# An attention and mixture-of-experts kernel: one small sum on another engine, three blocks in another buffer, and steps of the hand-written order moved

## The chip, the core and the metric

The kernel runs on one core of one Trainium2 chip. The metric is the device time of one execution in microseconds (us), the median of several runs. PE is the matmul engine (TensorE), DVE VectorE, ACT ScalarE, POOL GpSimd; SP only issues transfers. Each engine takes its instructions in the order in which the program lists them and stands at one whose inputs aren't ready.

## What is computed

The reference is multi-head attention with a learned bias from relative positions, followed by a mixture of experts in which each token goes to one expert (cut to what matters):

```python
scores = scale * q @ k.T + bias                      # 4 batches, 8 heads, 576 tokens, head size 64
attn = exp(scores - max(scores)); attn = attn / (sum(attn) + 1e-09)
x = (attn @ v) as [2304 tokens, 512]
logits = x @ w_gate                                  # 8 experts
e = argmax(logits); g = softmax(logits)[e]; o = sigmoid(x @ w_output_gate)[e]
out[token] = g * o * (maximum(x[token] @ w1[e], 0) @ w2[e])
```

## The kernel before

The program has three stages. The first computes the bias and is not touched. The second is attention: 4 batches of 4 pairs of heads, each pair one pass of the loop on line 997. The third is the experts' stage: slots of 288 tokens that share an expert, 8 of them always (`SURE`), more behind conditions.

**Attention.** What the loop issues, and in which order, stands in strings: `FIRST` for the first pass, `ORDER` for the middle ones, `LAST` for the last, `END` for what is left after it. An entry is a letter with a number: `s` makes the scores of one block of 128 rows for one head (matmuls on line 849, then `softmax_rows`: DVE adds the bias and finds the row's maximum on line 829, ACT takes the exponential on line 834 and writes the row sums to `sums`); `t` transposes weights in pieces of 128x128 on PE (lines 886, 898) and copies them from PSUM to `et` (lines 890, 901) on ACT or DVE, by the letter at its end; `a` multiplies them with `v` (line 918, twenty matmuls) and copies the result to `xt` (line 919). A minus sign means the pair before, a plus sign the pair after. All transposes and small products draw their PSUM tile from `psum_t()`, three buffers in rotation; the scores have two buffers of their own (`ps_s`).

**The queue of small work.** `w` and `u` in the strings, and the entries of `SLOT_WORK` in the experts' stage, each call `do_work`, which takes one step of the first generator in `rows`, or else in `work`. A step is the code up to the next `yield`. Behind the last pair of a batch three kinds of generator are queued: `emit_logits` (three per batch; the first of them, `qq == 0`, also makes the reciprocals of the softmax sums, lines 593 and 594; its copy `ls` on line 609 is ACT's), `emit_route` (gate and expert of each token; at its end it queues `emit_x`), and `route_group`, which turns the experts' numbers into lists of row indices for gathering and scattering. It runs once for batches 0 to 2 (part 0) and once for batch 3 (part 1). Its index matmuls are on line 413; their factors are `a2`, made on POOL for part 0 (lines 399 to 404), and `bl`, made on DVE (line 407).

**The x blocks.** `emit_x` transposes a batch's result into five blocks of rows (four of 128, one of 64), multiplies each on DVE by its gate (line 660) and stores it to DRAM from ACT's queue; a block's store is issued in the step of the next block (line 662), the last one's in a step of its own (line 666). In the last batch all five blocks come from the pool `x_p`, tag `x`, two buffers. Slot answers draw from the same two buffers (`new_y`: answers 0 and 1 of a slot; answer 2 has `y2`).

**Into the experts' stage.** `X` in `LAST` issues three gathers of slot 0's rows on POOL (line 497). The eight `y` entries split slot 0's first weights: ACT makes the high half (line 539), POOL subtracts for the low half (line 540, 128x512, SBUF to SBUF). `x` entries are `transpose_x(0, c)`: three transposes of a chunk of slot 0's rows (line 515), a copy on ACT (516), a subtraction on DVE (517).

**A slot** (`body`) has eight groups f0 to f7 of twelve matmuls (line 1110, three PSUM buffers); behind each ACT makes `hh` (1112) and DVE `hl` (1113), and behind every even group `split` makes two halves of a piece of the second weights (ACT line 486, DVE line 487). Then come four output groups d0 to d3 of 24 matmuls (line 1133), each with an ACT copy into `yts[s % 2]` (line 1139). At the end twelve transposes (1152) and three copies (line 1155: DVE, ACT, DVE) give the slot's three answers, which POOL scatters to the output (line 1076). `yts` are two tiles of 128x4x288, in the places (`qt1`, `qs1`) of attention's keys and queries.

Of the kernel before, what the change touches and what calls it, by code (L numbers as in the profile page):

```python
# [9 lines left out]
F32 = mybir.dt.float32  # L10
# [4 lines left out]
ACTF = mybir.ActivationFunctionType  # L15
ALU = mybir.AluOpType
# [4 lines left out]
B, H, S, D = 4, 8, 576, 64  # L21
HID = 32
NPAIR = H // 2
DM, DFF, NE = 512, 1024, 8
# [3 lines left out]
CH = 288  # L28
# [30 lines left out]
)  # L59

END = (
    "t10a- t11d- a1d- x x w a2d- x w x "
)


# [5 lines left out]
ON_ACT = "210210000111121212102110310010201111"  # L71

SLOT_WORK = (
# [61 lines left out]
def attention_moe_kernel(  # L135
# [15 lines left out]
    nc = tc.nc  # L151
    V = nc.vector
# [5 lines left out]
    qx = ctx.enter_context(tc.tile_pool(name="qx", bufs=1))  # L158
    nat = ctx.enter_context(tc.tile_pool(name="nat", bufs=1))
    spl = ctx.enter_context(tc.tile_pool(name="spl", bufs=1))  # L160
    vp = ctx.enter_context(tc.tile_pool(name="vp", bufs=2))
    xt_p = ctx.enter_context(tc.tile_pool(name="xt", bufs=3))
    x_p = ctx.enter_context(tc.tile_pool(name="x", bufs=2))
# [21 lines left out]
    def psum_t():  # L185
        return ps_t.tile([128, 512], F32, name="pt", tag="t")
# [7 lines left out]
    def route_batch(b):  # L194
# [31 lines left out]
        for t in range(t0, t0 + 5):  # L226
# [2 lines left out]
                out=pm[:, t + 1, :], in0=oh[:, t, :], in1=pm[:, 0 if first else t, :], op=ALU.add  # L229
            )  # L230

    gidx = [const.tile([G, n], U32, name=f"gidx{i}") for i, n in enumerate((NGA, NG + 1))]
    sidx = [const.tile([G, n], U32, name=f"sidx{i}") for i, n in enumerate((NGA, NG + 1))]
    ids_a = const.tile([G, NGA], F32, name="ids_a")
# [20 lines left out]
    def route_group(part):  # L255

        if part == 0:
            yield
        P = V if part else nc.gpsimd
        t0, nt = ((0, NTA), (NTA, NT - NTA))[part]  # L260
# [17 lines left out]
            out=cmp, in0=each(rk[:, nt, :], [128, 8, 16]), in1=over(cn("thr"), [128, 8, 16]), op=ALU.is_gt  # L278
# [7 lines left out]
        for i in range(2):  # L286
            cmp = rt.tile([128, 8, 8], F32, name="cmp8", tag="bl")
            V.tensor_tensor(
                out=cmp, in0=cn("inc").rearrange("p (e f) -> p e f", e=8), in1=over(nch[:, i, :], [128, 8, 8]),
# [5 lines left out]
        if part:  # L295
            V.tensor_scalar(
                out=nb, in0=cn("slot")[:, 0:MORE + 1], scalar1=cinc[:, 7:8], scalar2=float(MORE),
                op0=ALU.add, op1=ALU.is_equal,
# [8 lines left out]
        for i in range(2):  # L307
            sl = rt.tile([1, ns, 8], F32, name="sl", tag="a2")
            V.tensor_tensor(
                out=sl, in0=each(cn("slot")[0:1], [1, ns, 8]),  # L310
# [5 lines left out]
        if part:  # L316
# [11 lines left out]
                out=late, in0=ea, scalar=16.0, in1=ea, op0=ALU.is_lt, op1=ALU.mult  # L328
# [55 lines left out]
        for u in range(nt // 5):  # L384
            us = slice(u * 5, u * 5 + 5)
            ge = rt.tile([128, 5, NG + 1], BF16, name="ge", tag="ge")[:, :, 0:ng + 1]
            V.tensor_tensor(
                out=ge, in0=each(pos[:, us], [128, 5, ng + 1]), in1=over(cn("gthr")[:, 0:ng + 1], [128, 5, ng + 1]),
                op=ALU.is_ge,
            )  # L390
            yield
            lo = rt.tile([128, 5], F32, name="lo", tag="lo")
            V.tensor_reduce(out=lo, in_=ge, op=ALU.add, axis=AX.X)
            V.tensor_scalar(out=lo, in0=lo, scalar1=-1.0, scalar2=-float(G), op0=ALU.add, op1=ALU.mult)
            V.tensor_tensor(out=lo, in0=lo, in1=pos[:, us], op=ALU.add)
            if part:
                yield
            a2 = rt.tile([128, 5, 2, NG], BF16, name="a2", tag="a2")[:, :, :, 0:ng]
            P.tensor_tensor(out=ge[:, :, 0:ng], in0=ge[:, :, 0:ng], in1=ge[:, :, 1:ng + 1], op=ALU.subtract)
            for i, nm in enumerate(("tokhi", "toklo")):  # L400
                P.tensor_tensor(
                    out=a2[:, :, i, :], in0=ge[:, :, 0:ng],
                    in1=each(cn(nm)[:, t0 + u * 5:t0 + u * 5 + 5], [128, 5, ng]), op=ALU.mult,
                )
            yield
            bl = rt.tile([128, 5, G], BF16, name="bl", tag="bl")
            V.tensor_tensor(out=bl, in0=each(lo, [128, 5, G]), in1=over(cn("j96"), [128, 5, G]), op=ALU.is_equal)
            yield
            yield
            pi = psum_t()  # L410
            for i in range(2):
                for t in range(5):
                    nc.tensor.matmul(
                        pi[0:G, i * 128:i * 128 + ng], lhsT=bl[:, t, :], rhs=a2[:, t, i, :],
                        start=t == 0, stop=t == 4,
                    )
            V.scalar_tensor_tensor(
                out=ids[:, 0:ng], in0=pi[0:G, 0:ng], scalar=64.0, in1=ids[:, 0:ng], op0=ALU.mult, op1=ALU.add
            )
            V.tensor_tensor(out=ids[:, 0:ng], in0=ids[:, 0:ng], in1=pi[0:G, 128:128 + ng], op=ALU.add)  # L420
            if u < nt // 5 - 1:
                yield
        if part:
            yield
            g, n = 3 * SURE_A, NG - 3 * SURE_A
# [155 lines left out]
    def emit_logits(b, qq):  # L581

        n = 256 if qq < 2 else 64
        pl = psum_t()
        for pr in range(NPAIR):
            nc.tensor.matmul(
                pl[32 * pr:32 * pr + 32, 0:n], lhsT=wgb[:, pr, :], rhs=xt_t[b, qq][:, pr, :],
                start=True, stop=True,
            )
        if qq == 0:  # L590
            rec_t[b] = st_p.tile([128, 5, H], F32, name="rec", tag="rec", bufs=2)
            rec = rec_t[b][:, 0:4, :]
            V.tensor_scalar(out=rec, in0=sums_t[b], scalar1=1e-9, scalar2=None, op0=ALU.add)  # L593
            V.reciprocal(out=rec, in_=rec)
        if qq == 2:

            for hl in range(2):
                nc.tensor.matmul(
                    pl[0:64, 256 + 4 * hl:260 + 4 * hl], lhsT=ident[:, hl * 64:hl * 64 + 64], rhs=sums4_t[b],
                    start=True, stop=True,  # L600
                )
            rec = rec_t[b][0:64, 4, :]
            V.tensor_scalar(
                out=rec.rearrange("p (a t) -> p t a", t=2), in0=pl[0:64, 256:264].rearrange("p (t a) -> p t a", t=2),
                scalar1=1e-9, scalar2=None, op0=ALU.add,
            )
            V.reciprocal(out=rec, in_=rec)
        ls = st_p.tile([128, 256], F32, name="ls", tag="ls", bufs=1)
        nc.scalar.copy(out=ls[:, 0:n], in_=pl[:, 0:n])
        yield  # L610
        if b == B - 2:
            yield
        pt = psum_t()
        if qq < 2:
            for i in range(2):
                nc.tensor.transpose(pt[:, i * 128:i * 128 + 128], ls[:, i * 128:i * 128 + 128], ident)
            lt = st_p.tile([128, 2 * H, 16], F32, name="lt", tag="ls", bufs=1)
            rb = rec_t[b][:, 2 * qq:2 * qq + 2, :].rearrange("p t h -> p (t h)")
            V.tensor_tensor(
                out=lt, in0=pt[:, 0:256].rearrange("p (h e) -> p h e", e=16), in1=each(rb, [128, 2 * H, 16]),  # L620
                op=ALU.mult,
            )
            t = b * 5 + 2 * qq
            V.tensor_reduce(
                out=logits[:, t:t + 2, :], in_=lt.rearrange("p (t h) e -> p t e h", t=2), op=ALU.add, axis=AX.X
            )
        else:
            nc.tensor.transpose(pt[0:64, 0:128], ls[:, 0:64], ident)
            lt = st_p.tile([128, 2 * H, 16], F32, name="lt", tag="ls", bufs=1)[0:64, 0:H, :]
            V.tensor_tensor(  # L630
                out=lt, in0=pt[0:64, 0:128].rearrange("p (h e) -> p h e", e=16),
                in1=each(rec_t[b][0:64, 4, :], [64, H, 16]), op=ALU.mult,
            )
            V.tensor_reduce(
                out=logits[0:64, b * 5 + 4, :], in_=lt.rearrange("p h e -> p e h"), op=ALU.add, axis=AX.X
            )
# [9 lines left out]
    def emit_x(b):  # L646

        stored = None
        for qb in range(5):
            n = 128 if qb < 4 else 64  # L650
            xt = xt_t[b, qb // 2]
            c0 = (qb % 2) * 128 if qb < 4 else 0
            pt = psum_t()
            for pr in range(NPAIR):
                nc.tensor.transpose(pt[0:n, pr * 128:pr * 128 + 128], xt[:, pr, c0:c0 + n], ident)  # L655

            p, tag = (spl, "hl"[qb // 2]) if qb % 2 and b < B - 1 else (x_p, "x")
            x = p.tile([128, H, D], F32, name="x", tag=tag)
            p3 = pt[0:n].rearrange("p (h d) -> p h d", h=H)
            V.tensor_tensor(out=x[0:n], in0=p3, in1=each(rec_t[b][0:n, qb, :], [n, H, D]), op=ALU.mult)  # L660
            if stored:
                nc.scalar.dma_start(**stored)
            r0 = b * S + qb * 128
            stored = dict(out=x_dram[r0:r0 + n, :], in_=x[0:n].rearrange("p h d -> p (h d)"))
            yield
        nc.scalar.dma_start(**stored)
# [392 lines left out]
    with ExitStack() as ctx:  # L1059
# [6 lines left out]
        w2l = [wr.tile([128, 2, DM], F32R, name=f"w2l{i}") for i in range(4)]  # L1066
        hh_all, hl_all = (hp.tile([128, 8, CH], F32R, name=t) for t in ("hh", "hl"))
        hh, hl = ([t[:, i, :] for i in range(8)] for t in (hh_all, hl_all))
        yts = [qx.tile([128, 4, CH], F32, name=f"yt{t}", tag=t) for t in ("qt1", "qs1")]

        few.append(xt_p.tile([128, 4, FEW], F32, name="few", tag="xt1", bufs=2))
        puts = []
# [183 lines left out]
```

## Time and profile before

| | us |
|---|---|
| median of three runs | 630.18 (629.33 to 630.48) |
| profiled execution, its own time | 629.59 |
| its span, first to last instruction | 627.7 |
| PE busy | 580.1 (92%) |
| DVE busy | 420.2 (67%) |
| ACT busy | 374.7 (60%) |
| POOL busy | 95.3 (15%) |

All times in the rows are from the start of the span. Attention ends and slot 0 begins at about 380 us; slot 1 begins at about 413, and each later slot takes 28 us. A busy PE is not a PE at its best: a matmul at half the granted clock counts as busy too.

### The profile page before, as it was taken

What the parts mean: (1) busy time and instruction counts of PE and PEld (TensorE: products, weight loads), DVE (VectorE), ACT (ScalarE), POOL (GpSimd) and SP (SyncE); (2) the same over time, 40 slices, a digit from 0 to 9 for tenths busy, and PEclk for the clock granted to TensorE, in tenths of its full rate; (3) what the DMA queues carried; (4) which work ended last, traced back from release to release, by engine and by line L of the source; (5) the groups of instructions that cost most, each with busy time, mean ns of one, the idle gap of its engine ahead of it and who ended that gap; (6) DMA issues with size and microseconds to landing.
All of it is one profiled execution on the core that took longest, in us unless ns stands there. A gap on an engine that the chain in (4) does not pass through costs nothing.

```text
span 627.7 us, 13542 instructions
## 1 busy us (share of the span) xinstructions
PE 580.1 (92%) x5070; PEld 491.8 (78%) x5070; DVE 420.2 (67%) x978; ACT 374.7 (60%) x770; POOL 95.3 (15%) x172
## 2 busy tenths in 40 slices
PE   5878899999999999999898969989999999999992
PEld 2323478877878878887777748979999999999992
DVE  6978676667777777774787675748777765555611
ACT  5788677777777767778666624434554454545410
POOL 1000000000010000100103371022404041220202
PEclk9988899999999999999999979999999999999997
DMA  6998975665458656664644763547566565745521
GB/s 141 227 204 204 231 154 117 142 143 114 103 116 194 148 119 138 136 168 104 138 127 99 260 216 107 165 132 255 175 206 206 169 208 163 222 159 193 172 69 47
DMA packets 99092, 100.26 MB, mean 160 GB/s; under 512 B 71319, under 2 KB 71575, under 8 KB 99016
## 3 DMA queue, kind: packets, MB, share of 16 engines
q1 hardware_dynamic: 93028, 84.93, 52.5%
q0 software_dynamic: 3232, 9.64, 4.8%
q10 hardware_dynamic: 2756, 4.72, 2.1%
q8 instruction: 42, 0.69, 0.5%
q14 instruction: 34, 0.28, 0.1%
HBM read 60.34 MB, written 9.50 MB: 111 GB/s over the span
## 4 chain that ended last, share of the span: by engine, by line
PE 34%; issue 10%; DVE 5%; ACT 2%; DMA 1%; POOL 1%; POOLq 0%; ACTq 0%; DVEq 0%
PE p L1133 12%; PE p L1110 12%; PE pa L918 3%; PE pt L886 2%; DVE e L829 1%; PE pt L1152 1%; DMA out_dram<-y,sidx 1%; PE pt L515 1%; DVE rec L593 1%; PE ps L849 1%; ACT et L890 1%; ACT e L834 1%; POOL out_dram L1076 1%; ACT qt L802 0%; PE pt L655 0%
## 5 line engine op out<-in xcount | busy, mean ns | idle before, releaser
L834 ACT ACTIVATE e<-e,nm 128x576 f32<-128x576 f32 x144 | 111.3, 774 | 48.3 <-DVE nm L829 46.5
L829 DVE CUSTOM_DVE_ANT_0 e<-ps,bias 128x576 f32<-128x576 f32 x144 | 105.9, 752 | 34.1 <-PE ps L849 31.1
L1110 PE MATMUL p<-x,w 128*128 128x288 f32 x768 | 106.1, 297 | 2.8 <-DVE hl L1113 2.3
L1110 PEld LDWEIGHTS p<-x,w 128*128 128x128 f32 x768 | 102.8, 188 | 3.5 <-DVE hl L1113 2.7
L886 PE MATMUL pt<-kept,e 128*128 128x128 f32 x576 | 84.1, 280 | 8.3 <-DVE et L890 5.6
L886 PEld LDWEIGHTS pt<-kept,e 128*128 128x128 f32 x576 | 66.4, 143 | 23.9 <-issue 8.2
L849 PE MATMUL ps<-qt,qs 128*128 128x288 f32 x256 | 79.1, 328 | 3.4 <-DVE nm L829 2.1
L1133 PE MATMUL p<-hh,w2h 128*128 128x288 f32 x256 | 77.3, 302 | 0.0
L1133 PE MATMUL p<-hl,w2h 128*128 128x288 f32 x256 | 75.7, 296 | 0.5 <-DVE hl L1113 0.5
L1133 PE MATMUL p<-hh,w2l 128*128 128x288 f32 x256 | 75.5, 295 | 0.2 <-DVE w2l L487 0.2
L918 PE MATMUL pa<-et,vt 128*64 128x256 f32 (+1 forms) x640 | 74.4, 358 | 0.1
L890 ACT COPY et<-pt 128x512 f32<-128x512 f32 (+1 forms) x105 | 57.4, 565 | 23.1 <-PE pt L886 22.8
L849 PE MATMUL ps<-kl,qs 128*128 128x288 f32 x256 | 70.7, 294 | 0.0
L731 PE MATMUL pb<-hid,w2blk 128*32 128x288 f32 x576 | 49.5, 469 | 16.3 <-DVE hid L720 7.7
L918 PEld LDWEIGHTS pa<-et,vt 128*64 128x64 f32 x640 | 43.0, 138 | 22.8 <-issue 6.6
L849 PEld LDWEIGHTS ps<-qt,qs 128*128 128x128 f32 x256 | 48.3, 189 | 7.5 <-DVE nm L829 3.4
L1076 POOL DMA_INDIRECT out_dram<-y,sidx x22 | 25.7, 1170 | 180.9 <-DVE y L1155 150.8
L731 PEld LDWEIGHTS pb<-hid,w2blk 128*32 128x32 f32 x576 | 20.6, 121 | 41.3 <-DVE hid L720 10.0
L720 DVE TENSOR_SCALAR hid<-e,early 128x576 f32<-128x576 f32 x110 | 48.6, 514 | 5.2 <-ACT early L700 2.3
L1112 ACT ACTIVATE hh<-p 128x288 fp32r<-128x288 f32 x64 | 26.2, 411 | 41.6 <-PE p L1110 40.4
L487 DVE TENSOR_TENSOR w2l<-w2r,w2h 128x1024 fp32r<-128x1024 f32 x32 | 39.2, 1225 | 14.5 <-ACT w2h L486 14.5
L1133 PEld LDWEIGHTS p<-hl,w2h 128*128 128x128 f32 x256 | 48.1, 188 | 0.8 <-DVE hl L1113 0.8
(217 smaller groups left out, 978.2 us busy)
## 6 DMA issues: line engine op xcount, KB each, us to landing
w1r<-in_moe_w_dram SPq DMA_DIRECT2D x36, 512.0 KB, 3.8
w2r<-in_moe_w_dram SPq DMA_DIRECT2D x36, 512.0 KB, 3.9
kl<-qs SPq DMA_DIRECT2D x32, 288.0 KB, 5.1
nat<-in_k_dram SPq DMA_DIRECT2D x16, 288.0 KB, 3.9
nat<-in_q_dram SPq DMA_DIRECT2D x16, 288.0 KB, 5.1
bias<-evh SPq DMA_DIRECT2D x16, 288.0 KB, 4.2
bias<-evl SPq DMA_DIRECT2D x16, 288.0 KB, 5.2
qs<-qt SPq DMA_DIRECT2D x16, 288.0 KB, 3.2
```

The source lines that it names most:

```text
L487: V.tensor_tensor(out=lo, in0=src, in1=hi.bitcast(F32), op=ALU.subtract)
L720: V.tensor_scalar(out=to, in0=src, scalar1=bc[:, r:r + 1], scalar2=0.0, op0=ALU.add, op1=ALU.max,)
L731: nc.tensor.matmul(pb[32 * t:32 * t + 32, c, 0:288], lhsT=w2f, rhs=hids[t][:, c * 288:c * 288 + 288], start=True, stop=True,)
L829: V.tensor_tensor_reduce(out=e.rearrange("p (a j) -> p a j", a=2), in0=ps[:, :, 0:n], in1=bias_ap.rearrange("p (a j) -> p a j", a=2), scal ...
L834: nc.scalar.activation(out=e, in_=e, func=ACTF.Exp, scale=-1.0, bias=nm, accum_out=sum_ap)
L849: nc.tensor.matmul(ps[:, c, 0:288], lhsT=qs[:, o:o + 128], rhs=keys[:, k0 + c * 288:k0 + c * 288 + 288], start=n == 0, stop=n == 1,)
L886: nc.tensor.transpose(pt[:, n * 256 + j * 128:n * 256 + j * 128 + 128], es[j][:, (n0 + n) * 128:(n0 + n) * 128 + 128], ident,)
L890: copy(out=et[:, n0:n0 + nn, :].rearrange("p n s -> p (n s)"), in_=pt[:, 0:nn * 256])
L918: nc.tensor.matmul(pa[p:p + 64, 0:n], lhsT=values, rhs=weights, start=i == 0, stop=i == 4)
L1076: p = nc.gpsimd.indirect_dma_start(out=out, out_offset=bass.IndirectOffsetOnAxis(ap=idx, axis=0), in_=y[0:n], in_offset=None, bounds_check ...
L1110: nc.tensor.matmul(p1[:, 0:CH], lhsT=w[:, fs], rhs=x[:, c, :], start=n == 0, stop=n == 11)
L1133: nc.tensor.matmul(p2[:, 0:CH], lhsT=w[f // 2][:, f % 2, ds], rhs=x[f], start=n == 0, stop=n == 23)
```

## The change

1. Line 593: `sums + 1e-9` of each batch, 128x32, is an ACT instruction (Copy with a constant bias) instead of one of DVE. The reciprocal behind it stays on DVE. It runs four times.
2. `emit_x`: in the last batch, blocks 2, 3 and 4 lie in the buffer of the odd slots' answers, `yts[1]`: block 2 in its first 512 columns, block 3 in the next 512, block 4 in the first again. Blocks 0 and 1 keep the two buffers of `x_p`. `yts` becomes a list that is filled where the tiles were made.
3. `route_group`: one more `yield` ahead of the index matmuls, and none behind them between two sets. So a set's index matmuls come one step later, in the step of the next set's first instruction.
4. `END`: the four chunks of slot 0 are transposed in a row behind `a1d-`, and the two `w` are gone. `SLOT_WORK[0]` has an `f0` in front.

Where the steps of the last stretch go, worked out from the code:

| place | before | after |
|---|---|---|
| last pass, entries 6, 7 | index matmuls of set 2 of 3; next set | both in entry 7 |
| last pass, `u` behind `t20d-`, behind `t04d` | index matmuls of set 3; final indices | nothing of it; index matmuls of set 3 |
| last pass, next `u` | (empty) | final indices of part 0 |
| END, first `w`, second `w` | logits of batch 3, block 1, two steps | (no `w`) |
| slot 0, f0 to f3 | (none), block 2 of the logits, its second step, route 0 | block 1, its second step, block 2, its second step |
| slot 0, f4 to f7 | route 1 to route 4 | route 0 to route 3 |
| slot 0, d0 to d3 | x blocks 0, 1, 2, 3 | route 4, x blocks 0, 1, 2 |
| slot 1, f1, f3, f5, f7 | x block 4, last store, part 1 begins | x blocks 3, 4, last store, part 1 begins |
| end of part 1 | slot 3, d3 | slot 4, f1 |

```diff
 END = (
-    "t10a- t11d- a1d- x x w a2d- x w x "
+    "t10a- t11d- a1d- x x x x a2d- "
 )
 SLOT_WORK = (
-    "f1 f2 f3 f4 f5 f6 f7 d0 d1 d2 d3",
+    "f0 f1 f2 f3 f4 f5 f6 f7 d0 d1 d2 d3",
...
+    yts = []
...
             yield
             yield
+            yield
             pi = psum_t()
...
-            if u < nt // 5 - 1:
-                yield
...
-            V.tensor_scalar(out=rec, in0=sums_t[b], scalar1=1e-9, scalar2=None, op0=ALU.add)
+            nc.scalar.activation(out=rec, in_=sums_t[b], func=ACTF.Copy, bias=1e-9)
             V.reciprocal(out=rec, in_=rec)
...
-            p, tag = (spl, "hl"[qb // 2]) if qb % 2 and b < B - 1 else (x_p, "x")
-            x = p.tile([128, H, D], F32, name="x", tag=tag)
+            if b == B - 1 and qb > 1:
+                x = yts[1].rearrange("p a b -> p (a b)")[:, qb % 2 * DM:qb % 2 * DM + DM]
+                x = x.rearrange("p (h d) -> p h d", h=H)
+            else:
+                p, tag = (spl, "hl"[qb // 2]) if qb % 2 and b < B - 1 else (x_p, "x")
+                x = p.tile([128, H, D], F32, name="x", tag=tag)
...
-        yts = [qx.tile([128, 4, CH], F32, name=f"yt{t}", tag=t) for t in ("qt1", "qs1")]
+        yts.extend(qx.tile([128, 4, CH], F32, name=f"yt{t}", tag=t) for t in ("qt1", "qs1"))
```

## Rows read from the trace of the kernel before

**Rows 1.** The page, its head: the span; each engine's busy time, share, instructions.

```profile
span 627.7 us, 13542 instructions
...
PE 580.1 (92%) x5070; PEld 491.8 (78%) x5070; DVE 420.2 (67%) x978; ACT 374.7 (60%) x770; POOL 95.3 (15%) x172
```

**Rows 2.** Table by stretch: length, busy PE, PEld, DVE, ACT, POOL (instructions); clock, DMA, GB/s.

```profile
473.00:501.00 28.00, 28.00 (x225) 27.99 (x224) 20.72 (x44) 14.03 (x25) 6.52 (x6) 1.00 0.59 192
```

**Rows 3.** Waits of PE over the whole span: us in total, times, longest us.

```profile
PE pt L886 <- DVE et L890: 5.6, 1, 5.6
...
PE p L1110 <- DVE hl L1113: 2.3, 2, 2.1
...
PE pt L413 <- POOL a L401: 1.9, 2, 1.3
...
PE p L1133 <- DVE hl L1113: 0.5, 1, 0.5
PE p L1110 <- DVE x L517: 0.5, 1, 0.5
```

**Rows 4.** The chain that ended last, in order of time: start, us, what.

```profile
364.25 6.29 DVE rec L593
...
375.07 2.38 PE pa L918 x20
```

**Rows 5.** Timeline, 358 to 376, four engines: start, us, instruction, [idle before <- releaser].

```profile
358.12 2.56 POOL L540 TENSOR_TENSOR w<-w1r,w 128x512 fp32r<-128x512 f32 x2 [1.29 <-ACT w L539]
...
359.85 0.69 DVE L890 COPY et<-pt 128x512 f32<-128x512 f32 x1
...
364.34 6.14 POOL L540 TENSOR_TENSOR w<-w1r,w 128x512 fp32r<-128x512 f32 x5
...
364.86 0.66 PE L886 MATMUL pt<-kept,e 128*128 128x128 f32 x4
364.96 0.37 ACT L609 COPY ls<-pt 128x256 f32<-128x256 f32 x1 [1.67 <-PE pt L586]
...
370.83 0.63 DVE L890 COPY et<-pt 128x512 f32<-128x512 f32 x1
...
371.52 1.11 PE L886 MATMUL pt<-kept,e 128*128 128x128 f32 x4 [5.58 <-DVE et L890]
...
375.07 0.69 DVE L890 COPY et<-pt 128x512 f32<-128x512 f32 x1 [0.85 <-PE pt L886]
```

**Rows 6.** Table by stretch, PE alone: length, busy (instructions), granted clock, DMA, GB/s.

```profile
368.00:369.00 1.00, 0.00 (x0) 0.50 0.31 123
```

**Rows 7.** The tile `xg`, 355 to 384: the gathers' time from issue to landing.

```profile
DMA to landing us min/median/max: 3.0/4.0/4.9
```

**Rows 8.** Timeline of ACT in slot 0: the last logits copy.

```profile
385.84 0.21 ACT L609 COPY ls<-pt 128x64 f32<-128x64 f32 x1 [1.17 <-DVE rec L603]
```

**Rows 9.** Timeline around line 593 in batch 0: DVE and ACT.

```profile
139.72 0.17 DVE L593 TENSOR_SCALAR rec<-sums 128x32 f32<-128x32 f32 x1
...
139.93 0.35 DVE L594 RECIPROCAL rec<-rec 128x32 f32<-128x32 f32 x1
...
140.61 0.35 ACT L609 COPY ls<-pt 128x256 f32<-128x256 f32 x1
...
140.72 0.76 DVE L829 CUSTOM_DVE_ANT_0 e<-ps,bias 128x576 f32<-128x576 f32 x1 [0.43 <-PE ps L849]
```

**Rows 10.** Timelines at the end of slot 0: ACT's queue, DVE, ACT, PE.

```profile
411.16 0.33 ACTq L662 DMA_DIRECT2D x_dram<-x  x1
...
415.09 1.28 DVE L1155 COPY y<-pt 96x512 f32<-96x512 f32 x2 [2.87 <-DMA x_dram<-x]
...
418.99 0.58 ACT L1155 COPY y<-pt 96x512 f32<-96x512 f32 x1 [7.49 <-DMA out_dram<-y,sidx]
...
420.42 1.85 PE L1110 MATMUL p<-x,w 128*128 128x288 f32 x12 [2.06 <-DVE hl L1113]
```

**Rows 11.** Line 662, the x stores: time from issue to landing.

```profile
DMA to landing us min/median/max: 2.1/3.6/5.2
```

## The prediction

> **What bounds it now.** I read the page first: PE is busy 580.1 us of a span of 627.7 [rows 1], so the question is where PE's missing time lies. Next the table by stretch: in the experts' stage it doesn't lie, since a slot of 28 us there has 28.00 us of PE at the full granted clock [rows 2]; slots 2 to 6 all read so. Work that shifts about inside those slots changes nothing. Then PE's waits, longest first [rows 3]. Those of the bias stage are untouched by the change. What it can touch is one wait of 5.6 us for a copy of `et`, two of 2.3 together for `hl`, two of 1.9 together for the index factors, and two of 0.5. Last the chain of work that ended last: behind the 5.6 us stands a DVE instruction of line 593 that took 6.29 us [rows 4]; in batch 0 the same line took 0.17 [rows 9].
>
> The timeline of that place shows why [rows 5]. On POOL five subtractions of line 540 run in a row for 6.14 us, from 364.34 to 370.48, and the addition on DVE ends with them, at 370.54. Not all of DVE is held beside POOL: the copy of line 890 at 359.85, out of PSUM, took its usual 0.69 us in the middle of two subtractions. What is held is an addition with input and output in SBUF. Behind it in DVE's queue stands the copy that gives PE one of its three transpose buffers back, and PE stands from 365.94 to 371.52. A second loss follows: in the idle time TensorE's granted clock has gone to 0.50, 1.2 of 2.4 GHz [rows 6], and the four transposes after it take 1.11 us where four before it took 0.66 [rows 5].
>
> The Trainium skill, page "SBUF — State Buffer", section "Who interferes with whom", has a rule for this: copy, cast and tensor_scalar can take a pair of SBUF ports that VectorE shares with GpSimd, and whichever of the two comes second is blocked until the other's instruction is over. By that rule one subtraction would be waited for, not five; the trace agrees with it in kind and not in length.
>
> **Part by part, against the profiled execution: 629.59 us, 1.89 of it around the span. It lies 0.59 under the median of the runs, 630.18.**
>
> *1. The addition on ScalarE, last batch.* ACT is idle for 1.67 us, from 363.29 to its copy at 364.96 [rows 5]; its addition runs there and costs nothing. DVE is free for the reciprocal at 364.25 and needs 0.35 (as in [rows 9]). The transposes for the held copy end at 365.52 and the copy takes 0.63 [rows 5], so the buffer is free at 366.15, not 371.46: 5.3 us. Up to 375.76, where the last copy of `et` for the next matmul group ended, ran 4.30 us of DVE's copies, with 1.0 us of DVE waiting for PE at half clock in them (0.85 of it in the last row of [rows 5]). At full clock 3.3 us are left: that copy ends at 369.45. Twelve of the twenty matmuls of line 918 need it, 1.4 of their 2.38 us [rows 4]; they end at 370.9, not at 377.45. **−6.5**, bounds −5.3 (the clock gives nothing back) and −6.9. Next come the gathered rows: POOL's gathers are out before its subtractions at 364.34, the longest landing here took 4.9 us [rows 7], so 369.2, in time by 1.7. POOL's last subtraction, at 370.5, is needed only inside slot 0's first group, after 373.
>
> *2. The addition on ScalarE, batches 0 to 2.* On DVE it lies beside an idle piece of 0.43 us. On ACT it queues behind an exponential and its sum, to 140.61 in batch 0 [rows 9]. With 0.2 us for it (a copy of 64 columns takes 0.21 [rows 8]) the reciprocal starts near 140.85, not 139.93, and DVE's next `e` some 0.5 us late. Two more blocks of scores queue behind that one; PE has two buffers for them and would wait about 0.1 us at first. **+0.2** each, **+0.6**; bounds 0 and +0.9 each (all of 139.93 to 140.85 on PE).
>
> *3. Slot 0's four chunks in a row.* Their transposes need a fourth buffer where there are three: the fourth chunk waits for the first one's subtraction on DVE, some 0.5 us. That stands where slot 0's first group waits 0.5 for the same subtractions today [rows 3]. The last batch's middle logits aren't saved, they go behind slot 0's first two groups. POOL's queue keeps its order, gather 1 still after the subtractions. **0**, bounds −0.5 and +0.5.
>
> *4. All that follows, a step later.* In slot 0 the last logits step falls behind an even group, whose weight split DVE does first. ACT's copy of the logits waits for DVE's small sum already today, 1.17 us [rows 8], and one PE transpose waits for ACT: I expect a new wait there. Against it the routing leaves DVE freer at the end of the hidden stage, where PE waits 0.5 for `hl` [rows 3]. **0**, bounds −0.7 and +0.9. In slots 1 to 4 the steps only shift; DVE has some 7 us free in each [rows 2]. The indices are then done at slot 4's second group; the first gather that reads them follows its eighth.
>
> *5. x blocks in the odd answers' buffer.* Today DVE's first answer waits 2.87 us for an x store, and ACT's second one 7.49 us, until the first has been scattered. ACT's queue holds slot 1's `hh` behind it, and PE stands 2.06 us, then a little more, for `hl` [rows 3, 10]. After the change the second answer needs only the second block's store, which goes out where the third's does today, at 411.16. That landed by 415.1 [rows 10]; so the answer is out at 415.7, and PE wants `hl` at 418.4. **−2.3**, bounds 0 and −2.3. The new wait: the fifth block takes the third one's place, two groups (3.2 us) after that one's store went out, with slot 1's `hl` queued behind it on DVE. A store lands in 2.1 to 5.2 us [rows 11], and PE's three buffers let DVE stand about 2 us for nothing. The buffer's own answers come some 6 us after the last store.
>
> *6. Index matmuls a step later.* The longer of the two waits, 1.3 us, stays: its new step is the very next entry of the order, with no PE work between. The third set moves behind four score matmuls and two transposes, out of the 0.6 us wait [rows 3], but a later transpose then waits for another copy of DVE. **0**, bounds −0.6 and +0.4.
>
> Sum: −6.5 + 0.6 − 2.3 = **−8.2**, so 621.4 for the profiled execution and **622.0** against the median. A further stretch at half clock that comes or goes is worth some 1.4 us, by the one above.
>
> **Rivals.**
> A. *The reciprocal is held in the addition's place.* It too goes from SBUF to SBUF, and no row shows one beside a subtraction. Against it: its 0.35 us is twice the addition's time for the same 32 columns, so it doesn't run in the same way. Part 1 brings nothing: −1.7, 628.5. Chance 0.06. (The skill's section above names copy, cast and tensor_scalar, and no reciprocal.)
> B. *Only one subtraction's worth of the hold, 1.2 us, belongs to the addition*; the rest has a cause of its own and stays: −2.9, 627.3. For it: the other four subtractions started while the addition already stood. Against it: the hold ended 0.06 us after the fifth. Chance 0.03. (This is what the skill's rule of one instruction would leave.)
> C. *The second answer still gets the first one's buffer* and waits for its scatter, as today. Against it: today the fourth block's store isn't issued by then; with the change the two blocks in that pair of buffers are stored before. −5.9, 624.3. Chance 0.05.
> D. *Slower: DVE stands at the fifth x block* until the third one's store has landed. Past some 5 us each further us is a us of PE; it cancels the gain only past 13 us, and of 16 stores the longest took 5.2. With 15 us: 632. Chance 0.03.
> E. *ACT's turn comes late in the last batch*, its casts held by weights that are still loading, and DVE waits at the reciprocal instead: about 630. ACT's idle 1.67 us speak against it. Chance 0.03.
>
> **The numbers.** About 0.2% (1.26 us) is what a measurement of this kernel can tell from no change. The forecast has 0.80; its bounds, not all falling one way, give −10.8 to −4.6. The range is that, 619.4 to 625.6, and C lies in it; A, B, D and E are left out. Faster by over 0.2%: the forecast, A, B and C, 0.94. Within 0.2%: E, 0.03. Slower: D, 0.03.
>
> **What would show it.** Right: no DVE instruction over 2 us near 364, a reciprocal of 0.35 while POOL subtracts; PE's wait of 5.6 gone, its clock at 1.00 from there to slot 0; slot 1 without the 2.06; slots 2 to 6 still at 28 us. In batches 0 to 2 the reciprocal 0.9 us later. A new PE wait in slot 0 for `ls`. Wrong: a reciprocal of 6 us (A) or 5 (B), an answer that waits for a scatter (C), an x product that waits for its store (D); or a gain over 11, by which the clock or slot 0 gave more than I found.

## The result, and the profile after

The changed kernel takes **619.88 us** (median of 4 runs, 619.17 to 619.95); the kernel before, run beside it, 629.90 (629.33 to 630.48). The ratio is **0.9838**, 95% interval 0.9821 to 0.9855: 10 us faster, where 8.2 were forecast; the median lies inside the forecast's range, 0.5 us above its lower end. The profiled execution took 619.93 us.

The head of the page of the changed kernel, to be held against [rows 1]:

```profile
span 617.8 us, 13534 instructions
...
PE 576.8 (93%) x5070; PEld 489.2 (79%) x5070; DVE 413.1 (67%) x974; ACT 375.2 (61%) x774; POOL 94.7 (15%) x172
```

DVE has four instructions fewer and ACT four more: the additions, one for each batch. DVE's busy time falls by 7.1 us. That is not 7 us of arithmetic: an addition that is held counts as busy.

PE's waits in the changed kernel, those that answer to [rows 3] (us in total, times, longest):

```profile
PE pt L415 <- POOL a L402: 1.3, 1, 1.3
...
PE pt L628 <- ACT ls L609: 0.7, 1, 0.7
...
PE pt L515 <- DVE x L517: 0.5, 1, 0.5
...
PE pt L890 <- DVE et L894: 0.4, 1, 0.4
```

The wait of 5.6 for `et` is 0.4, the waits for `hl` are gone, one of the two for the index factors is left, and the one for `ls` is new. Those of the scores for `nm` grew from 2.1 in total to 3.0.

The timeline of the last batch, DVE, ACT, POOL and PE, beside [rows 5] (start, us, instruction, idle before and its releaser):

```profile
362.34 0.22 ACT L593 ACTIVATE rec<-sums 128x32 f32<-128x32 f32 x1
...
363.31 0.34 DVE L594 RECIPROCAL rec<-rec 128x32 f32<-128x32 f32 x1
...
363.38 6.19 POOL L540 TENSOR_TENSOR w<-w1r,w 128x512 fp32r<-128x512 f32 x5
...
364.69 0.69 DVE L894 COPY et<-pt 128x512 f32<-128x512 f32 x1 [1.04 <-PE pt L890]
...
365.44 0.66 PE L890 MATMUL pt<-kept,e 128*128 128x128 f32 x4 [0.36 <-DVE et L894]
...
365.74 0.60 DVE L624 TENSOR_REDUCE logits<-lt 128x32 f32<-128x256 f32 x1
...
367.88 0.69 DVE L894 COPY et<-pt 128x512 f32<-128x512 f32 x1 [0.15 <-PE pt L890]
```

POOL's five subtractions are there as before, 6.19 us, and the reciprocal runs its 0.34 at their beginning. The copy of `et` ends at 365.38, and the four transposes behind it take 0.66, with the granted clock at 1.00. In the chain of work that ended last, the matmul group that follows stands at

```profile
367.92 2.38 PE pa L922 x20
```

and ends at 370.30, where before it ended at 377.45 [rows 4].

The end of slot 0, queue and instructions of ACT, DVE and PE in the timeline, beside [rows 10]:

```profile
403.62 0.33 ACTq L666 DMA_DIRECT2D x_dram<-x  x1
...
405.42 1.28 DVE L1159 COPY y<-pt 96x512 f32<-96x512 f32 x2 [0.73 <-PE pt L1156]
...
407.46 0.58 ACT L1159 COPY y<-pt 96x512 f32<-96x512 f32 x1 [3.51 <-DMA x_dram<-x]
...
408.38 0.46 DVE L1117 SCALAR_TENSOR_TENSOR hl<-p,hh 128x288 fp32r<-128x288 f32 x1 [1.68 <-ACT hh L1116]
...
408.98 3.44 PE L1114 MATMUL p<-x,w 128*128 128x288 f32 x24
```

DVE's answer no longer waits for a store. ACT's second one waits for the second block's store, 3.8 us after that was issued, and no longer for a scatter. PE goes into the next group with no wait.

**Where the 9.9 us of span came from**, by the start of the same instruction in both timelines, or by its end in the chain where that is said:

| place | before | after | difference | since the place above |
|---|---|---|---|---|
| logits matmuls of batch 0, line 586 | 138.93 | 139.58 | +0.65 | +0.65 (bias stage; nothing changed yet) |
| second set of index matmuls | 342.62 | 343.14 | +0.52 | -0.13 (+0.16 of part 2, -0.29 of part 6) |
| the transposes after them | 347.29 | 346.22 | -1.07 | -1.6 (clock) |
| last key block's scores | 354.26 | 353.39 | -0.87 | +0.2 (part 6) |
| end of the twenty matmuls | 377.45 | 370.30 | -7.15 | -6.3 (part 1) |
| slot 1, start | 412.89 | 405.35 | -7.54 | -0.4 (work that now comes later) |
| slot 1, first output group | 429.63 | 419.68 | -9.95 | -2.4 (part 5) |
| end of the span | 627.7 | 617.8 | -9.9 | 0.0 |

The line on the clock is no part of the forecast's sum. The table by stretch (PE: length, busy and instructions, granted clock, DMA share, GB/s) reads in the kernel before

```profile
345.00:346.00 1.00, 1.00 (x8) 0.50 0.91 246
```

and in the changed one

```profile
345.00:346.00 1.00, 1.00 (x12) 1.00 0.37 66
```

Both traces have an idle time of PE of 1.3 us for the index factors just ahead of it, after which the clock fell to 1.2 GHz in one and stayed at 2.4 in the other. The experiments tell whether the change did that.

### The profile page after: what moved, and what is told of

It reads as the page before. It is cut to its first block, busy times and chain, and to the rows that moved or that the text cites. A ratio compares the mean times of both kernels' runs of the same rounds, so it can differ in the third digit from the quotient of the medians.

```text
span 617.8 us, 13534 instructions
## 1 busy us (share of the span) xinstructions
PE 576.8 (93%) x5070; PEld 489.2 (79%) x5070; DVE 413.1 (67%) x974; ACT 375.2 (61%) x774; POOL 94.7 (15%) x172
## 4 chain that ended last, share of the span: by engine, by line
PE 76%; issue 6%; DVE 6%; DMA 5%; ACT 4%; POOL 1%; POOLq 0%; SPq 0%; DVEq 0%; ACTq 0%
PE p L1114 15%; PE p L1137 15%; PE pa L922 13%; PE ps L853 9%; PE pt L890 9%; PE pb L735 2%; PE ps L869 2%; PE pt L803 2%; DVE e L833 2%; DMA bias<-evh 2%; DVE hid L724 2%; PE pt L655 1%; PE pt L1156 1%; PE pt L902 1%; PE pt L515 1%
## 5 line engine op out<-in xcount | busy, mean ns | idle before, releaser
L890 PE MATMUL pt<-kept,e 128*128 128x128 f32 x576 | 82.8, 277 | 2.8 <-ACT et L894 1.2
L1137 PEld LDWEIGHTS p<-hh,w2h 128*128 128x128 f32 x256 | 48.0, 188 | 0.6 <-issue 0.6
```

Of the source, the lines that this page charges most:

```text
L890: nc.tensor.transpose(pt[:, n * 256 + j * 128:n * 256 + j * 128 + 128], es[j][:, (n0 + n) * 128:(n0 + n) * 128 + 128], ident,)
L1137: nc.tensor.matmul(p2[:, 0:CH], lhsT=w[f // 2][:, f % 2, ds], rhs=x[f], start=n == 0, stop=n == 23)
```

## The experiments

Three sets of four, each with runs of the kernel before on the same chip. That kernel scattered more in them than beside the changed kernel (medians 630.29, 630.88 and 630.62, single runs from 627.2 to 635.8), so a difference under 2 us is read from a trace or not at all.

### One part of the change at a time

**e1_sum**: the kernel before with the addition on ScalarE alone.

```
-            V.tensor_scalar(out=rec, in0=sums_t[b], scalar1=1e-9, scalar2=None, op0=ALU.add)
+            nc.scalar.activation(out=rec, in_=sums_t[b], func=ACTF.Copy, bias=1e-9)
```

> The kernel before with the small sum on ScalarE alone. Theory (parts add up; the sum was held by POOL's five subtractions): the reciprocal takes 0.35 us beside them, PE's wait of 5.6 us is gone, -6.3 us, 623.6, with the 2.1 us at slot 1's start still there. Rival (the reciprocal had only been lucky, or the gain needs the moved steps): a wait of over 3 us stays. By my part 2 as predicted the three other batches would cost 0.6 us; by the changed kernel's trace they cost 0.0 to 0.2.

Measured 623.93 us, ratio 0.9895 (0.9848 to 0.9941). Its timeline (DVE, POOL) and its waits of PE:

```profile
364.24 0.34 DVE L594 RECIPROCAL rec<-rec 128x32 f32<-128x32 f32 x1
...
364.39 6.18 POOL L540 TENSOR_TENSOR w<-w1r,w 128x512 fp32r<-128x512 f32 x5
...
PE p L1110 <- DVE hl L1113: 2.0, 1, 2.0
...
PE pt L886 <- DVE et L890: 0.4, 1, 0.4
```

The wait for `et` goes with the addition alone; the wait for `hl` stays, and in this execution the clock fell behind it, in slot 1: from 416 to 417 us it was 0.50. Of the eight profiles that have this wait of some 2 us, five show such a stretch of 3 to 4 us at half clock behind it (e1, e3, e8, e9, e10) and three don't (before, e4, e6).

**e2_blocks**: the kernel before with the last x blocks in the odd answers' buffer alone.

```
-            p, tag = (spl, "hl"[qb // 2]) if qb % 2 and b < B - 1 else (x_p, "x")
-            x = p.tile([128, H, D], F32, name="x", tag=tag)
+            if b == B - 1 and qb > 1:
+                x = yts[1].rearrange("p a b -> p (a b)")[:, qb % 2 * DM:qb % 2 * DM + DM]
+                x = x.rearrange("p (h d) -> p h d", h=H)
+            else:
+                p, tag = (spl, "hl"[qb // 2]) if qb % 2 and b < B - 1 else (x_p, "x")
+                x = p.tile([128, H, D], F32, name="x", tag=tag)
```

> The kernel before with the x blocks 2 to 4 of the last batch in the odd answers' buffer alone. Theory: the second answer waits only for an x store, slot 1's wait for hl is gone, -2.3 to -2.5 us, 627.5; the 5.6 us wait stays. Rival (the gain comes from the later steps, which have fewer stores open at the end of slot 0): the answer waits for a scatter again, 629.9.

Measured 627.48 us, ratio 0.9943 (0.9911 to 0.9976). PE's waits, and ACT's second answer in its timeline:

```profile
PE pt L891 <- DVE et L895: 5.5, 1, 5.5
...
414.07 0.58 ACT L1160 COPY y<-pt 96x512 f32<-96x512 f32 x1 [1.57 <-PE pt L1157]
```

The mirror of e1: the long wait stays, the 2.3 us for `hl` in slot 1 are gone (the 0.5 of the other line stays), and the answer waits for PE's transposes alone. From slot 1's start (413.89) to its first output group (427.85) this trace has 13.96 us, that of the kernel before 16.74.

**e3_order**: the kernel before with the four chunks in a row and all that follows a step later, alone.

```
 END = (
-    "t10a- t11d- a1d- x x w a2d- x w x "
+    "t10a- t11d- a1d- x x x x a2d- "
...
-    "f1 f2 f3 f4 f5 f6 f7 d0 d1 d2 d3",
+    "f0 f1 f2 f3 f4 f5 f6 f7 d0 d1 d2 d3",
```

> The kernel before with the four chunks in a row and the step at f0 alone (x blocks in the two old buffers). Theory: 0, 629.9 within 0.7: slot 0's waits change places (0.5 at the fourth chunk, 0.7 for ls, none for hl at the end of the hidden stage), slot 1 still waits 2 us. Rival (the order is what paid): -1 us or more.

Measured 629.93 us, ratio 0.9996 (0.9963 to 1.0030). PE's waits:

```profile
PE p L1110 <- DVE hl L1113: 2.2, 1, 2.2
...
PE pt L628 <- ACT ls L609: 0.7, 1, 0.7
...
PE pt L515 <- DVE x L517: 0.5, 1, 0.5
```

The wait for `ls` is new, the two of 0.5 of [rows 3] are gone or have changed place: no gain shown.

**e4_index**: the kernel before with the index matmuls a step later, alone.

```
             yield
             yield
+            yield
             pi = psum_t()
...
-            if u < nt // 5 - 1:
-                yield
```

> The kernel before with the index matmuls a step later alone. Theory: 0, 629.9 within 0.6; the 1.3 us wait for the second set's factors stays. If the granted clock doesn't fall behind that wait (as it did at 344 to 347 before, and did not in the changed kernel), up to -1.6. Rival (the later step is what spares the half-clock stretch): -1.6 in every round, and a clock of 1.00 from 341 to 350 in this profile.

Measured 630.20 us, ratio 0.9982 (0.9961 to 1.0003). The waits for the index factors fall from 1.9 in two to 1.3 in one, and those of scores for `nm` grow from 2.1 to 3.2 in total: no gain shown. From the last logits matmuls of batch 2 to the second set of index matmuls the trace has 42.58 us, where the kernel before has 42.85.

**e5_back**: the changed kernel with the addition back on DVE, the edit of e1 reversed.

> The changed kernel with the small sum back on VectorE. Theory: line 593 is held for some 6 us again in the last batch and PE waits 5.6: +6.3 us, 626.2. Rival (the moved steps alone keep DVE and POOL apart): less than +3.

Measured 625.61 us, ratio 0.9934 (0.9912 to 0.9957). Its timeline and waits:

```profile
367.00 6.28 DVE L593 TENSOR_SCALAR rec<-sums 128x32 f32<-128x32 f32 x1
...
PE pt L890 <- DVE et L894: 5.5, 1, 5.5
```

The hold is back with the addition. The two ratios that share the change between them, e1's 0.9895 and e5's 0.9934, multiply to 0.983, inside the changed kernel's own interval.

**The clock near 345.** The windows of three of these kernels that hold the same wait of 1.3 us, in the table by stretch for PE, just after it: e3,

```profile
345.00:346.00 1.00, 1.00 (x8) 0.50 0.59 111
```

e5,

```profile
347.00:348.00 1.00, 1.00 (x8) 0.50 0.34 94
```

and e2, whose code is that of the kernel before up to here:

```profile
346.00:347.00 1.00, 1.00 (x14) 1.00 0.62 66
```

Half clock in the first two, full in the third. Of the twelve profiles that have this wait, four show the half clock behind it (before, e3, e4, e5) and eight don't (the changed kernel, e1, e2, e6 to e10). The kernel before's code up to here stands on both sides: before and e3 on the one, e2, e8, e9 and e10 on the other. So the 1.6 us of the table are a matter of the run. So is the +0.65 of its first line: over all the profiles the logits matmuls of batch 0 start anywhere from 138.2 to 142.0 us.

### What is held, and for how long

**e6_two_inputs**: the kernel before with the addition as an instruction with two inputs, both from SBUF; the value is the same.

```
-            V.tensor_scalar(out=rec, in0=sums_t[b], scalar1=1e-9, scalar2=None, op0=ALU.add)
+            V.scalar_tensor_tensor(out=rec, in0=sums_t[b], scalar=1e-9, in1=sums_t[b], op0=ALU.add, op1=ALU.max)
```

> The kernel before with the sum on VectorE in another form: scalar_tensor_tensor, (sums + 1e-9) max sums, the same numbers, two inputs in SBUF. If only the one-input form with input and output in SBUF (tensor_scalar) is held, it takes 0.2 us beside the subtractions and the time is 623.6. If two inputs in SBUF are held too (as the Trainium skill's page SBUF - State Buffer says against a GpSimd instruction that reads SBUF), it takes 1.2 us (one subtraction) or 6.3 (all five): 628.8 or 629.9.

Measured 630.78 us, ratio 1.0000 (0.9972 to 1.0028). Timeline, DVE and POOL:

```profile
363.34 6.35 DVE L593 SCALAR_TENSOR_TENSOR rec<-sums 128x32 f32<-128x32 f32 x1
...
363.49 6.15 POOL L540 TENSOR_TENSOR w<-w1r,w 128x512 fp32r<-128x512 f32 x5
```

The second input makes no difference: held just as long.

**e7_no_sum**: the changed kernel without the addition; the reciprocal reads the sums.

```
-            nc.scalar.activation(out=rec, in_=sums_t[b], func=ACTF.Copy, bias=1e-9)
-            V.reciprocal(out=rec, in_=rec)
+            V.reciprocal(out=rec, in_=sums_t[b])
```

> The changed kernel without the small sum: the reciprocal reads the sums. A sum is at least 1, so adding 1e-9 changes no float32. Theory: the reciprocal's wait of 1.05 us for ACT in batches 0 to 2 costs PE nothing, so 619.9 within 0.4. Rival (my part 2 as predicted): -0.6.

Measured 618.93 us, ratio 0.9823 (0.9790 to 0.9855). The reciprocal, beside the same five subtractions:

```profile
362.68 0.34 DVE L593 RECIPROCAL rec<-sums 128x32 f32<-128x32 f32 x1
...
362.78 6.20 POOL L540 TENSOR_TENSOR w<-w1r,w 128x512 fp32r<-128x512 f32 x5
```

The interval overlaps that of the changed kernel, measured in another set of runs: ScalarE's addition costs nothing that the times can tell. The traces tell more. From the first logits of batch 2 to the second, the three profiles with ScalarE's addition (the changed kernel, e1, e11) have 11.37 to 11.39 us, all the others 11.22 to 11.24: it costs some 0.16 us there.

**e8_pause**: the kernel before with the two last weight splits moved behind other steps, meant to break the row of subtractions.

```
-    "t02a a1a- y s5 X t00d w y s4 u a2d- y t14d y a0d w t13d u y t21d u y t12d u t20d "
+    "t02a a1a- y s5 X t00d w y s4 u a2d- y t14d y a0d w t13d u t21d u t12d u t20d y y "
```

> The kernel before with the last two of the eight weight splits moved behind the last pass's last transposes, so that POOL has three subtractions in a row and then a pause. Theory (VectorE gets in only when POOL's next instruction isn't waiting): line 593 takes 3 x 1.23 = 3.7 us instead of 6.3, PE's wait is 3.0, -2.6 to -3.2 us, 627. Rival (a hold of one instruction and another cause of 5 us): 6.3 us as before, 629.9.

Measured 630.21 us, ratio 0.9998 (0.9977 to 1.0019). A miss:

```profile
361.77 6.37 DVE L593 TENSOR_SCALAR rec<-sums 128x32 f32<-128x32 f32 x1
...
361.95 6.15 POOL L540 TENSOR_TENSOR w<-w1r,w 128x512 fp32r<-128x512 f32 x5
```

There was no pause. The steps between are DVE's copies; ACT, which hands POOL its input, had no more to do there and went straight on to the two splits. The next two put the splits behind a step with ACT's work in it.

**e9_three**: the same two splits moved further, to behind the first step of the list that follows, so that three are left in the row. One run.

```
-    "t02a a1a- y s5 X t00d w y s4 u a2d- y t14d y a0d w t13d u y t21d u y t12d u t20d "
+    "t02a a1a- y s5 X t00d w y s4 u a2d- y t14d y a0d w t13d u t21d u t12d u t20d "
-    "t10a- t11d- a1d- x x w a2d- x w x "
+    "t10a- y y t11d- a1d- x x w a2d- x w x "
```

> As e8_pause, which made no pause: ACT ran the two late splits at once, since all copies between them were DVE's. Here the last two of the eight splits stand behind the first transposes of the last stage (t10a-), whose ACT copy has to wait for PE and so for DVE. POOL then has three subtractions in a row and an empty queue behind them. If VectorE gets in as soon as POOL has no instruction ready, line 593 takes 3 x 1.23 = 3.7 us and PE's wait is 3.0; if the hold had another cause of its own, 6.3 again.

It took 628.86 us. Timeline (DVE, POOL) and wait of PE:

```profile
363.12 3.90 DVE L593 TENSOR_SCALAR rec<-sums 128x32 f32<-128x32 f32 x1
...
363.27 3.71 POOL L540 TENSOR_TENSOR w<-w1r,w 128x512 fp32r<-128x512 f32 x3
...
PE pt L886 <- DVE et L890: 3.1, 1, 3.1
```

**e10_none**: all five splits moved there. One run.

```
-    "t02a a1a- y s5 X t00d w y s4 u a2d- y t14d y a0d w t13d u y t21d u y t12d u t20d "
+    "t02a a1a- y s5 X t00d w s4 u a2d- t14d a0d w t13d u t21d u t12d u t20d "
-    "t10a- t11d- a1d- x x w a2d- x w x "
+    "t10a- y y y y y t11d- a1d- x x w a2d- x w x "
```

> As e9_three, with all five splits behind t10a-, so that POOL's queue is empty when VectorE reaches the sum. Theory: line 593 takes 0.2 us, up to 0.9 if the gather's issue holds it too; PE's wait is gone. The subtractions then end later, and slot 0's first group may wait for them. Rival (the last batch's sum is slow by itself): 6.3.

It took 624.66 us. The same views:

```profile
363.09 0.92 POOL L497 DMA_INDIRECT xg<-x_dram,gidx  x1 [0.30 <-issue]
...
363.88 0.17 DVE L593 TENSOR_SCALAR rec<-sums 128x32 f32<-128x32 f32 x1
...
369.09 6.24 POOL L540 TENSOR_TENSOR w<-w1r,w 128x512 fp32r<-128x512 f32 x5 [5.08 <-ACT w L539]
...
PE pt L886 <- DVE et L890: 0.4, 1, 0.4
```

The addition takes 6.3 us beside five subtractions, 3.9 beside three and 0.17 beside none, and PE's wait goes with it: 5.6, 3.1, 0.4. Only the place of the weight splits, ACT's half of them and POOL's, was changed between these three, so the hold is shown, and its length is that of the whole row. ACT's casts don't make it: in e9 none runs from 363.27 to 367. Nor does every instruction of POOL: in e10 the addition lies beside a gather's issue (363.09 to 364.01) and takes its 0.17. In e9 it ends 0.04 us after the third subtraction (363.27 + 3.71 = 366.98; 363.12 + 3.90 = 367.02).

### Three steps in other places

**e11_places**: the changed kernel with three steps in other places, for the three small waits that it has left. A `u` of the routing goes behind the attention step `a0d-`, so that PE has work before the index matmuls; the fourth chunk goes behind `a2d-`; and in slot 0 the third step of small work goes behind group 1, an odd one without a weight split, instead of group 2.

```
-    "b- B W s2 s1 c w u a0d- t10a- s3 u w t11a- s0 u t12a- s6 t20d- u s7 u g- t04d u t01d y t03a s8 u y "
+    "b- B W s2 s1 c w a0d- u t10a- s3 u w t11a- s0 u t12a- s6 t20d- u s7 u g- t04d u t01d y t03a s8 u y "
-    "t10a- t11d- a1d- x x x x a2d- "
+    "t10a- t11d- a1d- x x x a2d- x "
-    "f0 f1 f2 f3 f4 f5 f6 f7 d0 d1 d2 d3",
+    "f0 f1 f1 f3 f4 f5 f6 f7 d0 d1 d2 d3",
```

> The changed kernel with three steps moved, to take out the three waits of PE that are left around slot 0: the second set's index matmuls behind the next twenty av matmuls (1.3 us), the fourth chunk behind the last av group (0.5), the last logits step at f1 instead of f2 (0.7). If PE bounds these places: -2.5, 617.4, and no half-clock stretch near 345. Rival (something else is late there by about as much): under -1.

Measured 617.83 us, ratio 0.9797 (0.9764 to 0.9830). The waits of 1.3 us for the index factors, 0.7 for `ls` and 0.5 for `x` are gone from its list.

**e12_places_no_sum**: e11 with the edit of e7.

> e11_places without the small sum (the reciprocal reads the sums; a sum is at least 1, so 1e-9 changes no float32). Theory: ACT's sum costs nothing, so as e11_places within 0.3. Rival (the reciprocal's wait for ACT costs what I first took): -0.6.

Measured 616.78 us, ratio 0.9782 (0.9755 to 0.9809): the fastest. The 1.05 us to e11 were not expected, and the two intervals overlap. In the two profiles most of it has nothing to do with the addition: the logits of batch 0, ahead of the first addition, start at 141.63 us in e11 and 140.57 in e12, which is 1.06 of the 1.3 us between their spans (616.6 and 615.3).

Both beat the kernel before. The changed kernel was timed in another set of runs; its ratio of 0.9838 (0.9821 to 0.9855) lies clear of e12's and overlaps e11's. From the logits of batch 0 to the end of the span, past what scatters in the bias stage, its profile has 478.2 us and e7's 477.9, those of e11 and e12 475.0 and 474.7. Between these two marks none of the four shows half clock but in the last 10 us, so the 3 us can be put down to the three steps, with one execution of each.

## Why the prediction was right, step by step

**Part 1, the addition in the last batch: right, -6.3 for -6.5.** The chain of reasons held link by link. The last batch begins 0.87 us earlier in the changed trace; with that added back, the buffer is free at 366.25 (forecast 366.15) and the twenty matmuls end at 371.2 (370.9). The hold is the addition's (e1 takes it away, e5 brings it back), and it is made by the row of subtractions (e9, e10). The transposes behind it went back to 0.66 us, so the second loss, the clock, was rightly counted in. In the timeline of the kernel before the held addition reads

```profile
364.17 6.36 DVE L593 TENSOR_SCALAR rec<-sums 128x32 f32<-128x32 f32 x1
```

where the chain [rows 4] has 364.25 and 6.29: it leaves out the overlap with the copy ahead of it.

**Part 2, the additions of batches 0 to 2: the term that was mis-sized.** Forecast +0.6, measured +0.15, all of it in batch 2. The changed kernel's timeline in batch 0, ACT and DVE:

```profile
141.26 0.21 ACT L593 ACTIVATE rec<-sums 128x32 f32<-128x32 f32 x1
...
141.51 0.35 DVE L594 RECIPROCAL rec<-rec 128x32 f32<-128x32 f32 x1 [1.05 <-ACT rec L593]
...
141.78 0.69 DVE L833 CUSTOM_DVE_ANT_0 e<-ps,bias 128x576 f32<-128x576 f32 x1
...
142.40 0.75 DVE L833 CUSTOM_DVE_ANT_0 e<-ps,bias 128x576 f32<-128x576 f32 x1
```

and the second `e` of the kernel before:

```profile
141.80 0.76 DVE L829 CUSTOM_DVE_ANT_0 e<-ps,bias 128x576 f32<-128x576 f32 x1 [0.32 <-PE ps L849]
```

What was said of ACT and DVE came true: the addition queues on ACT, DVE waits 1.05 us for it, and the next `e` is late. Measured from the logits matmuls, that `e` starts after 2.20 us (141.78 - 139.58) where before it started after 1.79 (140.72 - 138.93): 0.41 late, 0.5 forecast. But the second one, at 142.40, starts after 2.82 us, before after 2.87 (141.80 - 138.93): the delay has been taken up by the idle pieces that DVE had ahead of the first `e`, 0.43 [rows 9], and ahead of the second, 0.32. PE shows no wait there. The forecast had counted the first idle piece and passed the rest on to two more blocks without looking for DVE's next one. From batch 0 to batch 1, and from 1 to 2, the differences between the two traces change by -0.02 and +0.01. In batch 2, from the first logits to the second, 11.23 us became 11.39 (e7 tells that this is the addition's).

**Parts 3 and 4, four chunks in a row and all a step later: right, about 0.** The new wait for `ls` came, and took what the others gave back. The timeline of PE in slot 0:

```profile
381.90 0.30 PE L628 MATMUL pt<-kept,ls 128*64 128x128 f32 x1 [0.70 <-ACT ls L609]
```

e3 shows the exchange by itself. The 0.4 us of the table ahead of slot 1 are no gain: PE's idle time in that stretch is 1.37 us before and 1.33 after, but its busy time falls from 34.07 to 33.72, since the transposes of the fourth x block now come behind slot 1's start.

**Part 5, the x blocks: the mechanism right, the gain larger than its bound.** Forecast -2.3, bounds 0 and -2.3; e2, which has the blocks alone, shows -2.8 (13.96 us for 16.74), and the changed kernel -2.4 with the fourth block's transposes added. The price was read from PE's 2.06 "then a little more" (2.3 in all); where the other half microsecond comes from is not shown. The second answer went out 3.8 us after the store that it needs, as before the first one did after its own (3.9); e2 shows it alone. The forecast's trace was also a mild case: in five of the eight profiles with this wait a stretch at half clock follows it (see e1), and the change takes that away as well.

**Part 6, the index matmuls: right, -0.1 for 0.** The wait of 1.3 stayed; the shorter wait was exchanged for others, as e4 shows too. They are not the one named: no transpose waits for a copy of DVE, but scores wait 0.92 us for `nm`, at 350.69, and the third set 0.35 for a copy of ACT. e11 shows what would have been needed: PE work between.

**The sum** came out 1.7 us short on the span (-9.9 for -8.2): 1.6 of clock, 0.45 of part 2 and 0.5 of part 5 on the one side, +0.65 of the bias stage and 0.2 of part 1 against them. The stretch at half clock was named ahead as something that may come or go, at 1.4 us. It went, in this pair of executions, by luck, and is not to be booked for the change.

**The rivals.** A fell with the reciprocal's 0.34 us. Input and output in SBUF, by which the forecast described the held instruction, are not enough for a hold: the reduction of line 624, from SBUF to SBUF, begins amid the subtractions in the changed kernel, at 365.74, and takes 0.60, where it took 0.59 before with no subtraction beside it. B fell with e9 and e10: all of the hold belongs to the row. The rule of the Trainium skill (page "SBUF — State Buffer", section "Who interferes with whom"), by which the second comer waits for one instruction of the other engine, was right in kind, that the addition stands still. The trace differs in two things: the length is 6.3 us for five and 3.9 for three, where one subtraction takes 1.28; and by the recorded starts the addition came first, by 0.08 to 0.18 us in the eight profiles that have it held. C fell, since ACT's answer waits for a store. D fell; of the three blocks in the new buffer the first, the third of the batch, waits for PE's transposes alone, and the other two, at 410.83 and 413.81, have no idle time ahead of them:

```profile
403.99 0.69 DVE L664 TENSOR_TENSOR ytqs<-pt,rec 128x512 f32<-128x512 f32 x1 [1.28 <-PE pt L655]
...
413.81 0.67 DVE L664 TENSOR_TENSOR ytqs<-pt,rec 64x512 f32<-64x512 f32 x1
```

E fell: ACT's addition begins at 362.34, DVE's reciprocal at 363.31, 0.75 us after the addition's end, with no idle time on DVE.

## What to carry to other kernels

A DVE instruction that takes many times its usual time is to be looked at in the timeline beside POOL: what counts is not the size of the held instruction but how many of POOL's subtractions run in a row beside it, and what is queued behind the held one on DVE. It is cured at either end: move the small operation to another engine or do without it, or move the row away. A buffer that the last stage doesn't need yet can take the place of the one whose store or scatter the next stage would wait for. And a delay that is put on an engine with idle pieces is followed to the next idle piece before it is priced.

## What was not expected of the hardware

- The hold lasts over the whole row of POOL's subtractions: 6.28 to 6.37 us beside five, 3.90 beside three. Between two of them DVE wasn't let in.
- The reciprocal, also from SBUF to SBUF, is not held in the same place: it starts 0.07 us ahead of the first subtraction (363.31, 363.38) and takes 0.34, where the addition of before started 0.17 ahead of it (364.17, 364.34) and took 6.36. No run has a reciprocal that begins in the midst of a subtraction, so that case stays open, and why the two differ as well.
- A reduction from SBUF to SBUF that begins amid the five subtractions is not held either: 0.60 us.
- The same idle time of 1.3 us is followed by half clock in 4 of 12 profiles, with the same code ahead of it on both sides, and that costs 1.6 us; the 2 us in slot 1 are followed by it in 5 of 8.
